# An S4D convolution with a gated feed-forward: the list scheduler replaced by one written-out order of all queues

## The chip, the cores and the metric

The kernel runs on one core of one Trainium2 chip. The metric is the device time of one execution in microseconds (us). Smaller is better. Three executions of the kernel before took 641.35, 641.83 and 646.14 us; their median is 641.83.

The core has five instruction streams that matter here: TensorE (PE, with its weight loads as PEld), VectorE (DVE), ScalarE (ACT), GpSimd (POOL) and SyncE (SP), which here mostly issues DMA transfers. Each engine runs its stream strictly in the order in which the program was built. Streams meet only at semaphores: an instruction whose input is not ready holds up everything behind it on its own engine.

## The reference

The input `x` (also `u`) has 2048 rows of 640 channels. One branch is a state-space convolution, the other a dense feed-forward of inner width 1728, and a gate per row mixes the two:

```python
dt = exp(log_dt); A = -exp(log_A_real) + 1j * A_imag
C = (C_real + 1j * C_imag) * dt[:, None]
P = exp((A * dt[:, None])[:, :, None] * pos)          # 640 x 128 x 2048
K = 2.0 * einsum("dn,dnl->dl", C, P).real             # convolution kernel
y = irfft(rfft(u_t, 2L) * rfft(K, 2L))[:, :, :L]      # causal convolution
a = y + u * D_skip
b = relu(B_x @ w1) @ w2                               # B_x: 2048 x 640
g = sigmoid((u * gate_w).sum(-1, keepdims=True))
out = g * a + (1 - g) * b
```

All inputs and the output are float32.

## The kernel before, in words

**Feed-forward.** Rows are worked on in blocks of 512 and 256. PE transposes an input block (`pk<-ident,xu`), ACT and DVE copy it out as a high part (ACT's CAST) and a low part (DVE) into the tile `xx`. Both weight matrices are split the same way, into `w1h`/`w1l` and `w2h`/`w2l`, and each product is made of three matmuls (high by high, low by high, high by low) in the accumulator `pf`, of which there are two banks. The hidden layer goes through ACT (`hh`, the ReLU) and DVE (`hl`, its low part); the second product is folded by DVE into the result tile `q`, which has two buffers. Feed-forward needs nothing of the other branch, so it is used as filler on PE from the first microsecond to the last.

**Generator.** To make the convolution kernel K, PE builds exponents in one bank (`pg<-tg,PS`, written by the visits of the queue `g`), ACT and DVE turn them into sines, cosines and magnitudes (`sc`, `mg`), DVE multiplies these into `G`, and PE contracts them into `pk` (the queue `gt`), from which DVE makes `kt`. `kt` goes through memory to `ck`. This fills the time from about 97 to 372 us.

**Convolution.** It is a Fourier transform in stages, one block of channels after another. PE's first stage is `pc<-ck,tf` for K (queue `sk`) and `pc<-xu,tf` for the input (queue `su`); the second stage is `pc<-ku,tm` and the second inverse `pc<-ku,tn` (both in the queue `s2`); the first inverse is `pc<-ku,tw` (queue `s4`). All write the accumulator `pc`, which has three banks. Between the stages DVE, ACT and POOL copy and multiply (`ku`, `kx`). After the last stage ACT empties `pc` with the gate into `yo` (two buffers), POOL adds, and transfers write the output. In the rest of this document a visit is one such task of PE.

**What sets the order.** Nothing is issued when it is written down. Every step is recorded as a task by `Plan.add` (L297), which names its engine, its queue, an estimated duration, the tasks that it depends on, the buffers that it takes (`take`) and those that it still reads (`use`). There are 2359 tasks in 57 queues. Within a queue the order is fixed. `Plan.run` (L344) then merges the queues: it keeps a model of each engine, looks at the head of every queue, and picks by rank. The rank is the one given at `add` plus a correction for each task number from the table `MOVES` (L265, made by `moves`, L135). Constants (L277 on) charge a change of kind on PE (`STICK`, and `CHANGE` in time) and the fetching of instructions (`FETCH`, `BUSY`, `STALL`). Where a task is picked its function runs and issues its instructions, so that the order of picks is the order on each engine.

All instructions are recorded by one helper (`Pinned.__getattr__`), so that the profile gives nearly all of them its line, L444; they are told apart by their tiles.

Of the kernel before, what the change touches and what calls it, by code (L numbers as in the profile page):

```python
# [25 lines left out]
S4R = 3  # L26
SKR = 2
SUR = 2
SKD = 2
SUD = 3  # L30
# [3 lines left out]
AHEAD = ()  # L34
HB = 1
XR = 2
XTR = 2
XT0 = 2
LATE_X = 1
LOGP = 0  # L40
LOGR = 3
JS2 = 0
JS1 = 0
JS4 = 0
STQ = 'SP'
STR = 4
TGR = 6
TGA = 4
TURNS = 2
G1R = 2  # L50
G4R = 3
LMR = 2
G5R = 0.5
GPR = 1
GTR = 3
S2D = 1
S2P = 2
RLR = 2
S4A = .5
PA = 3  # L60
PL = 2.5
YO = 2
YJ = 2
KRANK = 3

# [3 lines left out]

# [32 lines left out]

# [16 lines left out]
class Token:  # L119


    def __init__(self, ring):
        self.ring, self.users, self.left, self.free = ring, 0, 0, 0.0


class Ring:
    def __init__(self, n):
        self.n, self.slots = n, [0.0] * n

    def token(self):  # L130
        return Token(self)

def moves():  # L135
    r = {}
    for v, s in (
# [119 lines left out]
        for x in s.split():  # L257
            a, _, step = x.partition('/')
            a, _, b = a.partition('-')
            for i in range(int(a), int(b or a) + 1, int(step or 1)):  # L260
                r[i] = v
    return r


MOVES = moves()  # L265


# [1369 lines left out]
```

## Time and profile before

One execution was profiled. Its instructions span 642.3 us; the profile gives no other time of it. That is 0.5 above the median of the three timed runs, 641.83.

| | busy, us | share of the span | instructions |
|---|---|---|---|
| PE | 618.4 | 96% | 8676 |
| PEld | 493.1 | 77% | 8676 |
| DVE | 505.5 | 79% | 841 |
| ACT | 377.8 | 59% | 539 |
| POOL | 84.0 | 13% | 114 |

The mean clock that the throttle granted to PE is 0.992 of full. A busy PE need not be PE at its peak: matmuls are pipelined and the end of each is modelled, so rows of PE overlap, and what a matmul costs is read from the start of one row to the start of the next. In the rows a tile stands without its number, `out<-in`, with the part of the array that it uses, its shape and how many of the same kind follow each other; in brackets is the time that the engine idled just before, and what ended it. "issue" is idle time for which the profile shows no releaser.

### The profile page before, as it was taken

What the parts mean: (1) busy time and instruction counts of PE and PEld (TensorE: products, weight loads), DVE (VectorE), ACT (ScalarE), POOL (GpSimd) and SP (SyncE); (2) the same over time, 40 slices, a digit from 0 to 9 for tenths busy, and PEclk for the clock granted to TensorE, in tenths of its full rate; (3) what the DMA queues carried; (4) which work ended last, traced back from release to release, by engine and by line L of the source; (5) the groups of instructions that cost most, each with busy time, mean ns of one, the idle gap of its engine ahead of it and who ended that gap; (6) DMA issues with size and microseconds to landing.
All of it is one profiled execution on the core that took longest, in us unless ns stands there. A gap on an engine that the chain in (4) does not pass through costs nothing.

```text
span 642.3 us, 19948 instructions
## 1 busy us (share of the span) xinstructions
PE 618.4 (96%) x8676; PEld 493.1 (77%) x8676; DVE 505.5 (79%) x841; ACT 377.8 (59%) x539; POOL 84.0 (13%) x114
## 2 busy tenths in 40 slices
PE   7999999899999999999999999998999989899997
PEld 5999998888997887888898886666647645557666
DVE  4699946998999989999999957886757857858642
ACT  5455338999898987899889803131441452233541
POOL 0000000000000000000000000051340440532634
PEclk9899999999999999999999999999999999999999
DMA  9954974332346632533353269966139656454165
GB/s 241 284 221 148 277 238 139 106 110 102 109 133 210 230 128 94 199 124 108 112 187 116 79 195 261 266 144 136 32 78 271 177 155 145 174 134 135 59 187 141
DMA packets 75457, 102.56 MB, mean 160 GB/s; under 512 B 7529, under 2 KB 58601, under 8 KB 75114
## 3 DMA queue, kind: packets, MB, share of 16 engines
q1 hardware_dynamic: 74970, 100.39, 51.8%
q8 instruction: 68, 1.11, 0.7%
q10 hardware_dynamic: 400, 0.90, 0.5%
q14 instruction: 19, 0.16, 0.1%
HBM read 62.21 MB, written 39.06 MB: 158 GB/s over the span
## 4 chain that ended last, share of the span: by engine, by line
PE 60%; DVE 14%; ACT 13%; DMA 6%; issue 3%; SPq 2%; POOL 1%; DVEq 0%; ACTq 0%; POOLq 0%
PE pf L444 38%; PE pc L444 15%; ACT sc L444 5%; PE pk L444 4%; DVE sc L444 4%; DVE G L444 3%; DVE mg L444 3%; ACT L444 3%; PE pg L444 3%; SPq L444 2%; DMA out_dram<-yo 2%; ACT mg L444 2%; DMA xu<-in_A_u_dram 2%; ACT yo L444 1%; DMA part<-q 1%
## 5 line engine op out<-in xcount | busy, mean ns | idle before, releaser
L444 PE MATMUL pf<-xx,w1h 128*128 128x256 f32 (+1 forms) x760 | 190.8, 348 | 0.7 <-DVE w1h L444 0.4
L444 PEld LDWEIGHTS pf<-xx,w1h 128*128 128x128 f32 x760 | 125.5, 193 | 32.2 <-issue 16.5
L444 POOL TENSOR_TENSOR ku<-ku,kx 128x256 f32<-128x256 f32 x80 | 56.8, 735 | 488.6 <-ACT ku L444 422.4
L444 PE MATMUL pf<-xx,w1l 128*128 128x512 f32 (+1 forms) x340 | 117.1, 344 | 0.1
L444 ACT COPY ku<-pc 128x512 f32<-128x512 f32 (+1 forms) x60 | 43.9, 752 | 87.3 <-PE pc L444 87.2
L444 PE MATMUL pf<-w2h,hh 128*128 128x320 f32 x288 | 91.1, 320 | 1.2 <-issue 0.6
L444 PE MATMUL pf<-w2l,hh 128*128 128x320 f32 x288 | 87.7, 309 | 0.0
L444 DVE STREAM_TRANSPOSE ku<-pc 128x512 f32<-128x512 f32 x80 | 77.3, 1060 | 13.2 <-PE pc L444 13.0
L444 PE MATMUL pf<-w2h,hl 128*128 128x320 f32 x256 | 74.0, 315 | 0.0
L444 PEld LDWEIGHTS pf<-xx,w1l 128*128 128x128 f32 x340 | 65.7, 193 | 7.9 <-DVE w1l L444 0.3
L444 PEld LDWEIGHTS pf<-w2h,hh 128*128 128x128 f32 x288 | 54.0, 188 | 11.9 <-issue 9.2
L444 ACT ACT_TABLE_LOAD x42 | 53.9, 1283 | 4.1 <-DVE sc L444 3.3
L444 PEld LDWEIGHTS pf<-w2l,hh 128*128 128x128 f32 x288 | 54.1, 188 | 0.2
L444 DVE TENSOR_TENSOR mg<-mg,sc 128x1024 f32<-128x1024 f32 x40 | 48.9, 1223 | 2.4
L444 PEld LDWEIGHTS pf<-w2h,hl 128*128 128x128 f32 x256 | 46.3, 188 | 5.6 <-issue 5.1
L444 ACT COPY sc<-pg 128x1024 f32<-128x1024 f32 x40 | 40.4, 1010 | 16.0 <-PE pg L444 16.0
L444 DVE TENSOR_TENSOR sc<-sc,mg 128x1024 f32<-128x1024 f32 x40 | 48.8, 1219 | 0.0
L444 ACT ACTIVATE sc<-sc,half_pi 128x1024 f32<-128x1024 f32 x40 | 45.6, 1139 | 0.0
L444 ACT ACTIVATE hh<-pf 128x512 fp32r<-128x512 f32 (+1 forms) x40 | 20.3, 508 | 41.8 <-PE pf L444 41.8
L444 PE MATMUL pc<-ku,tm 64*32 64x256 f32 x1280 | 41.3, 380 | 3.4 <-issue 1.9
L444 DVE SCALAR_TENSOR_TENSOR hl<-pf,hh 128x512 fp32r<-128x512 f32 (+1 forms) x40 | 23.2, 580 | 26.6 <-ACT hh L444 15.8
L444 ACT ACTIVATE sc<-sc 128x1024 f32<-128x1024 f32 x40 | 42.2, 1055 | 0.2
(171 smaller groups left out, 1153.1 us busy)
## 6 DMA issues: line engine op xcount, KB each, us to landing
xx<-xt SPq DMA_DIRECT2D x24, 640.0 KB, 6.7
xt<-xx SPq DMA_DIRECT2D x16, 640.0 KB, 3.9
part<-q SPq DMA_DIRECT2D x16, 640.0 KB, 3.4
q<-part SPq DMA_DIRECT2D x16, 640.0 KB, 4.4
ws<-in_B_w_dram SPq DMA_DIRECT2D x20, 320.0 KB, 3.7
kd<-kt SPq DMA_DIRECT2D x80, 64.0 KB, 1.7
ck<-kd SPq DMA_DIRECT2D x40, 128.0 KB, 4.5
xu<-in_A_u_dram SPq DMA_DIRECT2D x10, 512.0 KB, 6.6
```

The source lines that it names most:

```text
L444: return lambda *a, **k: self._tc.keep_in_program_order(f(*a, **k))
```

## The change

`Plan.run` no longer decides anything. `QUEUES` gives each of the 57 queues a letter, and `ORDER` is a string that says from which queue the next task comes, with a count where several come in a row, 2359 steps in all. `run` walks through it, checks that each task's inputs are done and its buffers free in this order, and lets it issue. Durations, ranks, lags, `MOVES` and the constants are gone from the code, and `add` loses those arguments. The tasks, their dependencies, the buffers and their counts, and the order within each queue are the same, and so is the number of matmuls, vector operations and transfers. What differs is how the queues are merged.

```diff
+QUEUES = {
+    'a': 'ACT.ff', 'b': 'ACT.g', 'c': 'ACT.gw', 'd': 'ACT.mx', 'e': 'ACT.prma', 'f': 'ACT.prmc',
...
+    'B': 'DVE.z', 'C': 'PE.ff', 'D': 'PE.g', 'E': 'PE.gb', 'F': 'PE.gt', 'G': 'PE.s2', 'H': 'PE.s4',
+    'I': 'PE.sk', 'J': 'PE.su', 'K': 'POOL.mx', 'L': 'POOL.s2', 'M': 'POOL.s4', 'N': 'PY.open', 'O': 'SP.ck',
...
+ORDER = (
+    'C,N:R4,C,Ca,Cam,am,lmlAElACA3C2lCACA2amcCmC2amClmClA2CAl2CAaCamClmCAlU2CaACamCmB2CaBCB:CBCa;2C.CaQtftC2tC2tC'
...
-    def add(self, eng, q, dur, fn, deps=(), take=(), use=(), rank=5, mode=None, kb=0, port=False, n=0, late=False):
+    def add(self, eng, q, fn, deps=(), take=(), use=()):
...
     def run(self):
-        self.free = {e: 0.0 for e in self.LAG}
...
+        queues = {k: iter(self.queues.pop(tuple(x.split('.')))) for k, x in QUEUES.items()}
+        assert not self.queues, list(self.queues)
+        for n, k in re.findall(r'(\d*)(\D)', ORDER):
+            for _ in range(int(n or 1)):
+                t = next(queues[k])
+                assert all(d.done for d in t.deps), (k, n)
+                for b in t.take:
+                    b.ring.free -= 1
+                    assert b.ring.free >= 0, (k, n)
+                t.fn()
+                t.done = True
+                for b in (*t.take, *t.use):
+                    b.left -= 1
+                    b.ring.free += b.left == 0
+        assert not any(next(q, None) for q in queues.values())
```

Counted over the whole program by the queue of each task, PE's stream falls into 244 stretches of one kind before and 209 now: of feed-forward 113 and 88, of stage two and the second inverse (`s2`) 34 and 28, of `su` 16 and 14, of `sk` 14 and 11, of the first inverse (`s4`) 6 and 7; those of the generator (40 of `g`, 20 of `gt`) stay. A way from feed-forward into the convolution and back occurs 65 times before and 44 times now, one into the generator and back 46 and 42 times. The separate instructions that only wait for a semaphore are 174 and 206 on DVE, 106 and 93 on ACT, 153 and 158 on PE, 180 and 161 on SP, 87 and 90 on POOL. On SP the first weight load is now issued ahead of the first input load.

PE at the start of the program, before. `pg<-gw,ones` spreads the gate's weights over the partitions (queue `gb`), `pf<-xx,w1h` is the first hidden group of feed-forward:

```order
L444 MATMUL pg<-ident,xu 128x128 x2
L444 MATMUL pf<-xx,w1h_156 128x256 x10
L444 MATMUL pf<-xx,w1h_191 128x256 x2
L444 MATMUL pf<-xx,w1l_192 128x256
...
L444 MATMUL pk<-ident,xu 128x128 x4
L444 MATMUL pg<-gw,ones 128x512
L444 MATMUL pg<-gw,ones 128x128
L444 MATMUL pf<-xx,w1h_199 128x256 x2
```

The same place now:

```order
L186 MATMUL pg<-ident,xu 128x128 x2
L186 MATMUL pg<-gw,ones 128x512
L186 MATMUL pg<-gw,ones 128x128
L186 MATMUL pf<-xx,w1h_182 128x256 x10
L186 MATMUL pf<-xx,w1h_186 128x256 x2
L186 MATMUL pf<-xx,w1l_187 128x256
...
L186 MATMUL pk<-ident,xu 128x128 x4
```

The spreading moved from behind the next block's transposes to ahead of the first hidden group, directly behind the transposes that use the same bank `pg`.

PE in the convolution, from the second pair of first-inverse visits on (515 to 530 us of the profile), before. `tw` is the first inverse, `tn` the second, `ck,tf` and `xu,tf` the first stage of the next block of channels:

```order
L444 MATMUL pc<-ku,tw 64x512 x8
L444 MATMUL pf<-xx,w1h_5183 128x512 x2
L444 MATMUL pf<-xx,w1l_5184 128x512
L444 MATMUL pc<-ku,tn 64x128 x64
...
L444 MATMUL pc<-ck,tf 64x512 x4
L444 MATMUL pf<-xx,w1h_5210 128x512 x2
L444 MATMUL pf<-xx,w1l_5211 128x512
L444 MATMUL pc<-ck,tf 64x512 x4
L444 MATMUL pc<-xu,tf 64x512 x8
```

The same place now:

```order
L186 MATMUL pc<-ku,tm 32x256 x32
L186 MATMUL pc<-ku,tw 64x512 x4
L186 MATMUL pf<-xx,w1h_5192 128x512 x2
L186 MATMUL pf<-xx,w1l_5193 128x512
L186 MATMUL pc<-ku,tn 64x128 x64
L186 MATMUL pc<-ku,tw 64x512 x4
L186 MATMUL pc<-ck,tf 64x512 x8
...
L186 MATMUL pc<-xu,tf 64x512 x4
L186 MATMUL pc<-ck,tf 64x512 x8
```

The two first-inverse visits (`x8` is two of them) stand apart now, the second behind a feed-forward group and the second inverse, and the first-stage visits stand two and three together.

DVE in the generator, around 123 us of the profile, before. `G`, `mg` and `sc` are the generator's products, `hl` and `xx` feed-forward steps:

```order
L444 TENSOR_TENSOR kt<-kt,dsk 128x8
L444 SCALAR_TENSOR_TENSOR G<-mg,sc 128x16x32
L444 TENSOR_TENSOR G<-mg,sc 128x16x32
L444 TENSOR_TENSOR mg<-mg,sc 128x16x2x32
L444 SCALAR_TENSOR_TENSOR hl_1582<-pf,hh_1581 128x512
L444 TENSOR_TENSOR xx<-pk,xx 128x512
```

The same place now:

```order
L186 SCALAR_TENSOR_TENSOR G<-mg,sc 128x16x32
L186 TENSOR_TENSOR G<-mg,sc 128x16x32
L186 TENSOR_TENSOR kt<-kt,dsk 128x8
L186 SCALAR_TENSOR_TENSOR hl_1566<-pf,hh_1565 128x512
L186 TENSOR_TENSOR xx<-pk,xx 128x512
L186 SCALAR_TENSOR_TENSOR hl_1587<-pf,hh_1586 128x256
L186 TENSOR_TENSOR mg<-mg,sc 128x16x2x32
```

The two feed-forward steps moved ahead of the generator's product into `mg`.

At the end of the program the last two first-inverse visits of PE moved behind four more pieces of feed-forward. In the last block of channels a run of stage-two visits (`tm`) now follows a second inverse (`tn`) with nothing between.

More of the change, by code (lines that the diff above doesn't have):

```diff
@@ L1 @@
 import math
+import re
 from contextlib import ExitStack
@@ L560, in weights @@
             else:
-                a = A('SP', 'w', 1.2 if first and f else 0.62, load, after, take=[s_], kb=fn * (5 if first and f else 2.5), rank=1)
-            b = A('ACT', 'w', 0.63, high, [a], take=[w_], use=[s_], rank=1)
-            c = A('DVE', 'w', 0.75, low, [b], use=[s_, w_], rank=1, port=True)
+                a = A('SP', 'w', load, after, take=[s_])
+            b = A('ACT', 'w', high, [a], take=[w_], use=[s_])
+            c = A('DVE', 'w', low, [b], use=[s_, w_])
             wload[p, f, two] = a
@@ L870, in gates @@
             for k in range(17):
-                a = [A('DVE', 'gate', 0.16, rec.one(k, 17, go), a, rank=4)]
+                a = [A('DVE', 'gate', rec.one(k, 17, go), a)]
             self.gated = a[0]
@@ L1520, in copy @@
                         S.mul(o, st['p4', i, j][:, q, b], self.gate[:, b0 + b:b0 + b + 1])
-                c = A('ACT', 's4', 1.0, copy, [a], take=[x for x in (y_, g_ if first else None) if x],
-                      use=[b_] + ([g_] if g_ and not first else []), rank=S4A)
+                c = A('ACT', 's4', copy, [a], take=[x for x in (y_, g_ if first else None) if x],
+                      use=[b_] + ([g_] if g_ and not first else []))
                 self.need_gates.append(c)
```

409 lines of the change are left out of this document (122 added, 287 removed), and 124 rows, old and new, of tables (QUEUES, r).

## Prediction

> **What bounds the kernel now.** I read the profile in this order: the busy times and the chain of waits on the page, the busy times by stage, the table of what TensorE (PE) waited for, and then the timelines of the places that those point to. The page first: busy time and share by engine, then the chain that ended last by engine.
>
> ```profile
> PE 618.4 (96%) x8676; PEld 493.1 (77%) x8676; DVE 505.5 (79%) x841; ACT 377.8 (59%) x539; POOL 84.0 (13%) x114
> ...
> PE 60%; DVE 14%; ACT 13%; DMA 6%; issue 3%; SPq 2%; POOL 1%; DVEq 0%; ACTq 0%; POOLq 0%
> ```
>
> PE is the bound over the whole, yet 40% of the chain is something else, so one has to go by stage. The busy times in four stretches (the first loads, feed-forward alone, the stage that generates the convolution kernel, the convolution with its tail); the columns are length, then PE, weight load, DVE, ACT, POOL, clock, DMA share and GB/s:
>
> ```profile
> 0.00:23.00 23.00, 18.20 (x96) 16.07 (x97) 11.91 (x25) 10.76 (x20) 0.87 (x7) 0.85 1.01 259
> 23.00:97.00 74.00, 73.45 (x564) 72.50 (x562) 57.34 (x126) 33.96 (x71) 0.00 (x0) 1.00 0.70 225
> 97.00:372.00 275.00, 268.08 (x4255) 234.83 (x4259) 255.47 (x431) 243.81 (x273) 0.00 (x0) 1.00 0.40 134
> 372.00:640.00 268.00, 258.63 (x3784) 169.70 (x3772) 180.80 (x261) 89.28 (x176) 83.14 (x107) 0.99 0.58 161
> ```
>
> From 23 to 97 us PE is idle for 0.55 us: nothing to gain. From 97 to 372 PE (268.1 of 275), DVE (255.5) and ACT (243.8) are all nearly full, with DVE only 275 − 255.5 = 19.5 us from being the bound itself. From 372 on PE alone is full. The idle time that an order can remove is 23 − 18.2 = 4.8, 6.9 and 9.4 us in the other three. What PE waited for (total, times, longest):
>
> ```profile
> PE pc L444 <- issue: 3.6, 2, 1.9
> PE pc L444 <- ACT yo L444: 3.0, 2, 1.7
> PE pk L444 <- DVE xx L444: 3.0, 4, 1.4
> PE pk L444 <- DMA xu<-in_A_u_dram: 2.6, 2, 1.7
> PE pg L444 <- ACT mg L444: 2.4, 4, 1.2
> ```
>
> These five are 14.6 us. But a busy PE also hides what a change of kind costs, since a matmul's end is modelled and its row reads as busy. That cost shows in the starts of neighbouring rows.
>
> **Fewer changes of kind on PE.** The timeline of PE around 522 and 503 us (start, busy, instruction):
>
> ```profile
> 521.55 0.73 PE L444 MATMUL pf<-xx,w1h 128*128 128x512 f32 x2
> 522.12 0.40 PE L444 MATMUL pf<-xx,w1l 128*128 128x512 f32 x1
> 522.35 0.62 PE L444 MATMUL pf<-xx,w1h 128*128 128x512 f32 x2
> 522.81 0.40 PE L444 MATMUL pf<-xx,w1l 128*128 128x512 f32 x1
> 523.14 1.09 PE L444 MATMUL pc<-ck,tf 64*64 64x512 f32 x8
> 524.16 0.73 PE L444 MATMUL pf<-xx,w1h 128*128 128x512 f32 x2
> ...
> 502.50 1.96 PE L444 MATMUL pc<-ku,tm 64*32 64x256 f32 x64
> 504.39 0.42 PE L444 MATMUL pf<-w2l,w2h 128*128 128x320 f32 x1
> ...
> 507.67 1.09 PE L444 MATMUL pc<-ku,tm 64*32 64x256 f32 x32
> 508.69 0.74 PE L444 MATMUL pf<-xx,w1h 128*128 128x512 f32 x2
> ```
>
> Within feed-forward, two matmuls take 522.81 − 522.35 = 0.46 us from start to start; the two just after a convolution matmul take 522.12 − 521.55 = 0.57, so entering costs 0.11. A single one takes 522.35 − 522.12 = 0.23 before its like and 523.14 − 522.81 = 0.33 before a convolution visit, so leaving costs 0.10. One stage-two visit that feed-forward follows takes 508.69 − 507.67 = 1.02; two together take 504.39 − 502.50 = 1.89, so the first, with its like behind it, takes 0.87: 0.15 more. A round trip into the convolution and back is 0.11 + 0.10 + 0.15 = 0.36. By the order, the trips between feed-forward and convolution fall from 65 to 44: 21 × 0.36 = 7.6 at most. A trip whose place PE would have waited at anyway saves nothing; if that holds for two in five, 4.5 is left. Trips to the generator fall by 4 and count nothing here, with 4 × 0.36 = 1.4 as their upper bound. The waits listed above number 14 against 65 trips, so most trips don't stand at a wait: I take **−7.2**, bounds −4.5 to −9. The Trainium skill, in "TensorEngine Tiling (Array Packing)", Key Properties, says that a change of tiling mode drains TensorE; the rows agree in direction (128*128 to 64*64 and back), and the page has no price.
>
> **The start.** The timeline of PE from 11.9 to 21.6 us, with the idle time and its releaser in brackets:
>
> ```profile
> 11.91 0.28 PE L444 MATMUL pf<-xx,w1l 128*128 128x256 f32 x1
> ...
> 12.27 0.28 PE L444 MATMUL pf<-xx,w1l 128*128 128x256 f32 x1
> 14.23 0.63 PE L444 MATMUL pk<-ident,xu 128*128 128x128 f32 x4 [1.68 <-DMA xu<-in_A_u_dram]
> 14.79 1.83 PE L444 MATMUL pg<-gw,ones 1*128 1x512 f32 x4
> 16.55 0.80 PE L444 MATMUL pf<-xx,w1h 128*128 128x256 f32 x2
> ...
> 20.98 0.41 PE L444 MATMUL pf<-xx,w1l 128*128 128x256 f32 x1
> ...
> 21.62 0.41 PE L444 MATMUL pf<-xx,w1l 128*128 128x256 f32 x1
> ```
>
> The gate's broadcast takes 16.55 − 14.79 = 1.76 us and stands behind a wait of 1.68 for the next block of the input. Now it stands ahead of the first hidden group, so it fills that wait: −1.68, if its bank (written by transposes just before it, emptied by ACT and DVE) is free. On SP the first weight load is now issued ahead of the input; one issue on that queue takes about 0.6 (row below), so everything behind may come 0.6 later. After the wait a group of three matmuls takes 21.62 − 20.98 = 0.64 instead of 12.27 − 11.91 = 0.36: half the clock, for some (21.62 − 16.55)/0.64 = 8 groups, 8 × 0.28 = 2.2 us. Without the gap this should go at least in part; I take −1.9. Sum −1.68 + 0.6 − 1.9 = **−3.0**, bounds 0 to −3.9. The Trainium skill ("TensorE: Matmul & The Clock Gate", What's actually happening) lets the clock fall only after an idle window of about 3.4 us on a free-running grid. Here 1.68 us of waiting came before it, so gap and clock need not be tied as closely as I tie them; that is a rival below.
>
> **The convolution's banks.** PE at 525 us, and the two rows that bear on the tail:
>
> ```profile
> 525.05 1.09 PE L444 MATMUL pc<-ck,tf 64*64 64x512 f32 x8
> 527.83 1.95 PE L444 MATMUL pc<-xu,tf 64*64 64x512 f32 x16 [1.69 <-ACT yo L444]
> ...
> 612.57 0.62 SPq L444
> ...
> 624.57 4.59 DMA out_dram<-yo
> ```
>
> The two visits of the first inverse (pc<-ku,tw) stand together in before, take two of the three convolution banks, and ACT empties them one after the other (yo). Now a feed-forward group and two visits stand between the second and the first at this place, so ACT has the first bank empty when the second is written, and feed-forward follows before the next visit asks for a bank. Of the 3.0 us in the table I take **−2.0**, bounds −3.0 to +1. New close neighbours cost something: in the last block of channels the first stage-two visits (tm) now stand directly behind the second inverse (tn), and several stage-two visits stand in pairs where a feed-forward group lay between, so a bank or the input of a visit may come late. The trace shows no wait of such a pair; the nearest rows are the yo waits, 1.7 at the longest. One of those and half of another: **+2.5**, bounds 0 to +5.
>
> **The tail.** The last two first-inverse visits now stand behind four more pieces of feed-forward, each of three long matmuls (3 × 0.23 = 0.69): some 2.7 us later in PE's work. What hangs on them is a chain: output transfer (4.59 above), ACT, POOL, and DVE's step into q, for which PE already waits:
>
> ```profile
> PE pf L444 <- DVE q L444: 0.5, 2, 0.3
> ```
>
> So nothing covers this chain. It would end 2.7 later against PE's work, unless the visits' own transfers, which queue on SP at 0.62 an issue, find the queue emptier: **+1.3**, bounds 0 to +2.7.
>
> **The generator stage.** Around 123 us DVE does a long product of the generator ahead of the small step (xx) that PE's next transposes wait for; the first two rows are DVE's, the last is PE's:
>
> ```profile
> 122.47 1.23 DVE L444 TENSOR_TENSOR mg<-mg,sc 128x1024 f32<-128x1024 f32 x1
> ...
> 124.22 0.68 DVE L444 TENSOR_TENSOR xx<-pk,xx 128x512 fp32r<-128x512 f32 x1
> ...
> 124.95 0.44 PE L444 MATMUL pk<-ident,xu 128*128 128x128 f32 x2 [1.39 <-DVE xx L444]
> ```
>
> With the product behind xx, that wait falls by up to 1.23. xx itself needs ACT's copy, which runs beside the product:
>
> ```profile
> 122.47 0.58 ACT L444 CAST xx<-pk 128x512 fp32r<-128x512 f32 x1
> ```
>
> It ends at 123.05. DVE's hl step stays ahead of xx, and takes what lies between the two rows, 124.22 − 122.47 − 1.23 = 0.52, so that it is over before 123.05. So xx can start near 123.1 in place of 124.22: 1.0 earlier, with some room for what comes late. A second of the four waits in the table is taken to be of this kind. That is −1.9 of the 3.0. The waits for ACT's mg (2.4) fall where the generator's visits to PE, which share one bank, stand further apart; I leave the longest (1.2) as it is, since the order is the same there, and halve the rest: −0.6. Against these, DVE has 32 more waiting instructions than before (206 for 174), and behind each the generator's work queues in order: +0.5 taken. **−2.0**, bounds −4 to +2.
>
> **Instruction supply.** Two waits have no releaser but issue:
>
> ```profile
> 448.39 2.36 PE L444 MATMUL pc<-ku,tn 32*64 32x128 f32 x86 [1.75 <-issue]
> ...
> 548.56 1.75 PE L444 MATMUL pc<-ku,tm 64*32 64x256 f32 x56 [1.88 <-issue]
> ```
>
> Both break a run of small matmuls in the middle, where instructions are consumed fastest. The instruction set is the same and the small matmuls stand at nearly the same counts from the start, so I leave both: **0**, bounds −3.6 (both gone) to +3.8 (two more). The Trainium skill ("Runtime: NRT & Kernel Launch", Instruction fetch mechanics) says that fetching is hidden behind the issue of instructions; by it these waits would not be there, and denser runs would cost nothing. The rows speak against it, so longer stretches of small matmuls remain a danger.
>
> **Sum.** −7.2 − 3.0 − 2.0 + 2.5 + 1.3 − 2.0 + 0 = −10.4. The profiled execution spans 642.3 us: 642.3 − 10.4 = 631.9. The median of the runs is 641.83, 0.5 below that span, so the forecast is 631.5.
>
> **Rivals.** With this kernel about 1% (635.4 and 648.2) can be told from no change.
>
> 1. The new neighbours eat the gains of the waits. The two terms of −2.0 vanish and +2.5 and +1.3 stay: 642.3 − 7.2 − 3.0 + 3.8 = 635.9, so 635.4 as a median or a little above. For it: PE's waits move easily from one releaser to another, as five nearly equal ones show. Against: in the convolution feed-forward waits nowhere for long (of its waits only that for q, 0.3 at the longest, is shown there), so there is work to put between. Chance 0.16, within 1%.
> 2. The clock at the start stays halved, because it follows a window and not the gap. The start gives −1.1 in place of −3.0: 631.5 + 1.9 = 633.4. This is what the clock page's grid allows. Chance 0.12, faster.
> 3. Two more runs of small matmuls break for instructions: 631.5 + 2 × 1.9 = 635.3, and up to 637 with half a clock behind each. For it: longer stretches. Against: the same total in the same blocks. Chance 0.08, mostly within 1%.
> 4. Slower: DVE becomes the bound of the generator. It runs in order, and each of its 32 added waits can hold it for one ACT operation, whose mean is about 1.0 in the generator:
>
> ```profile
> L444 ACT COPY sc<-pg 128x1024 f32<-128x1024 f32 x40 | 40.4, 1010 | 16.0 <-PE pg L444 16.0
> ```
>
> 32 × 1.0 = 32 us against 19.5 us of slack: the stage grows by 12.5, its −2.0 is lost, and the gaps it opens on PE leave more feed-forward for the end. 631.5 + 12.5 + 2.0 = 646, and with the start's gain lost too 649. It decides from 0.6 us per added wait on. Against: before, 431 DVE instructions of the stage shared 19.5 us of idle time, 0.05 each, so that a wait is mostly met already. Chance 0.07, of which 0.05 slower by over 1%.
> 5. All terms near their good ends: 642.3 − 9 − 3.9 − 3 − 4 + 0 = 622.4, 624 being likelier. Chance 0.09, faster.
>
> That the change doesn't do what it says is ruled out: the order shows 209 stretches of one kind on PE where 244 were.
>
> **Numbers.** The forecast's own case has 0.48, with 628 to 635. Faster: 0.48 + 0.12 + 0.09 + a little of 1 and 3 = 0.71. Within 1%: 0.24. Slower: 0.05. The range 624 to 638.5 leaves out the slower rival, the far ends of 1, 3 and 5, and little else.
>
> **What would show it.** Right: between 10 and 20 us no wait of PE over 0.5 and the clock column at full by 20; the wait for ACT yo under 1 us in all; the wait for DVE xx near 1; the generator's end (the last pg matmul) some 5 us earlier; PE's busy time down by about 7 with the same number of matmuls. Wrong: DVE in the chain of waits well above 14%, PE waits in the generator above 7 us, a third and fourth wait for issue, or a wait of over 2 us in the last 20 us of PE.

## The result, and the profile after

The changed kernel takes 621.5 us (median of four runs, 620.6 to 622.7), the kernel before 641.7: a ratio of 0.969, 95% interval 0.965 to 0.973. It is 20.2 us faster, twice the 10.4 that were forecast, and 2.5 us below the forecast range. The profiled execution spans 619.5 us, 22.8 less than that of before. (`QUEUES` names 58 queues; the text above counts 57.) Here are the page of the kernel after (busy time by engine, then the chain that ended last), and its busy times by stage, with borders at the same places in the work as for before:

```profile
PE 605.9 (98%) x8676; PEld 492.8 (80%) x8676; DVE 505.9 (82%) x841; ACT 376.1 (61%) x539; POOL 83.9 (14%) x114
...
PE 76%; ACT 8%; DVE 7%; DMA 4%; issue 2%; SPq 1%; POOL 1%; ACTq 0%; DVEq 0%; POOLq 0%
```

```profile
0.00:23.00 23.00, 18.25 (x116) 17.02 (x117) 11.31 (x23) 12.56 (x24) 0.88 (x7) 0.93 0.95 250
23.00:94.00 71.00, 70.77 (x541) 70.15 (x540) 58.78 (x129) 31.67 (x67) 0.00 (x0) 1.00 0.60 201
94.00:362.00 268.00, 265.35 (x4242) 233.81 (x4244) 252.16 (x427) 243.26 (x273) 0.00 (x0) 1.00 0.45 144
362.00:617.00 255.00, 251.51 (x3793) 171.82 (x3785) 183.63 (x264) 88.56 (x176) 82.98 (x107) 1.00 0.61 171
```

PE's share of the chain rose from 60 to 76%: it is nearer to being the only bound. DVE does the same 506 us in a shorter time and did not become the bound of the generator. What PE waited for, after:

```profile
PE pg L186 <- DVE xx L186: 1.7, 1, 1.7
...
PE pg L186 <- ACT mg L186: 1.3, 2, 1.1
PE pk L186 <- DMA xu<-in_A_u_dram: 1.1, 1, 1.1
PE pc L186 <- issue: 1.0, 3, 0.5
PE pk L186 <- DVE xx L186: 0.9, 3, 0.5
PE pc L186 <- DVE ku L186: 0.8, 2, 0.5
PE pk L186 <- issue: 0.6, 2, 0.4
```

ACT yo is gone from the list (3.0 before), issue fell from 3.6 to 1.0 for `pc`, DVE xx for `pk` from 3.0 to 0.9.

Since both orders hold the same tasks, PE's time can be split task by task: the start of a task to the start of the next, less the shortest usual such time of tasks of the same make-up (their 5th percentile over both traces). What is left over is idle time that the trace shows, or a cost at a place where the next task is of another queue, or the rest (halved clock, and tasks that take longer than their best). In us:

| PE, us | before | after | difference |
|---|---|---|---|
| work at its usual best | 570.4 | 570.4 | 0 |
| idle: start and feed-forward alone | 3.9 | 3.5 | −0.4 |
| idle: generator | 6.9 | 2.7 | −4.3 |
| idle: convolution | 7.7 | 2.1 | −5.6 |
| changes of kind: convolution | 20.5 | 13.4 | −7.1 |
| changes of kind: elsewhere | 7.8 | 5.3 | −2.6 |
| rest | 19.2 | 16.4 | −2.8 |

The differences add up to 22.8; the 1.5 us ahead of PE's first matmul and the 4.4 from its last task on are the same in both and are left out. Some 45% of it is waits, and nearly as much is changes of kind. Of the last two rows 2.3 belong to the first 25 us, that is, to the clock (below).

### The profile page after: what moved, and what is told of

Read it like the earlier page. It is cut to its first block, busy times and chain, and to the rows that moved or that the text cites. A ratio compares the mean times of both kernels' runs of the same rounds, so it can differ in the third digit from the quotient of the medians.

```text
span 619.5 us, 19956 instructions
## 1 busy us (share of the span) xinstructions
PE 605.9 (98%) x8676; PEld 492.8 (80%) x8676; DVE 505.9 (82%) x841; ACT 376.1 (61%) x539; POOL 83.9 (14%) x114
## 3 DMA queue, kind: packets, MB, share of 16 engines
q8 instruction: 68, 1.11, 0.8%
## 4 chain that ended last, share of the span: by engine, by line
PE 76%; ACT 8%; DVE 7%; DMA 4%; issue 2%; SPq 1%; POOL 1%; ACTq 0%; DVEq 0%; POOLq 0%
PE pf L186 51%; PE pc L186 15%; PE pk L186 6%; PE pg L186 4%; ACT sc L186 4%; DVE ku L186 3%; ACT L186 2%; SPq L186 1%; ACT mg L186 1%; DMA xu<-in_A_u_dram 1%; DMA ck<-kd 1%; DVE sc L186 1%; DVE mg L186 1%; DVE G L186 1%; DMA out_dram<-yo 1%
## 5 line engine op out<-in xcount | busy, mean ns | idle before, releaser
L186 PE MATMUL pf<-xx,w1h 128*128 128x256 f32 (+1 forms) x760 | 187.0, 344 | 0.0
L186 PEld LDWEIGHTS pf<-xx,w1h 128*128 128x128 f32 x760 | 124.9, 192 | 28.0 <-issue 13.4
L186 ACT ACTIVATE mg<-pg 128x1024 f32<-128x1024 f32 x40 | 41.7, 1043 | 0.2
L186 PE MATMUL pc<-ku,tm 64*32 64x256 f32 x1280 | 39.8, 379 | 0.6 <-DVE ku L186 0.5
```

The costliest lines, as they stand in the source:

```text
L186: return lambda *a, **k: self._tc.keep_in_program_order(f(*a, **k))
```

## The experiments

All are the changed kernel's code with another `ORDER` string (the order of before can be written as such a string too), two of them with one more edit, which is shown. A ratio is to the runs of before on the same chip.

| run | what | median, us | ratio, 95% interval |
|---|---|---|---|
| e_start | changed order up to the generator only | 642.5 | 1.002 (0.998 to 1.006) |
| e_gen | changed order in the generator only | 636.1 | 0.990 (0.986 to 0.994) |
| e_conv | changed order in the convolution only | 628.5 | 0.982 (0.976 to 0.987) |
| e_loads_later | before, two loads later | 638.4 | 0.995 (0.992 to 0.998) |
| e_no_loads_before | before, four loads left out | 638.0 | 0.993 (0.990 to 0.996) |
| e_after_again | the changed kernel again | 622.5 | 0.969 (0.966 to 0.972) |
| e_no_loads_after | changed, four loads left out | 620.1 | 0.965 (0.962 to 0.968) |
| e_loads_into_runs | changed, one load behind a store | 624.6 | 0.971 (0.966 to 0.976) |
| e_load_early | changed, one load earlier | 622.8 | 0.970 (0.967 to 0.973) |
| e_resplit | changed, 21 more trips | 630.9 | 0.980 (0.976 to 0.985) |
| e_dve_back | changed, DVE's products back | 623.3 | 0.971 (0.966 to 0.976) |
| e_yo_joined | changed, one pair of visits joined | 624.8 | 0.973 (0.971 to 0.975) |
| e_tail_back | changed, the tail's visits back | 625.4 | 0.974 (0.972 to 0.977) |
| e_gate_later | changed, gate's spreading later | 621.8 | 0.968 (0.964 to 0.973) |
| e_best | changed, two places mended | 619.7 | 0.965 (0.963 to 0.967) |

### The three stages, each alone

```diff
 e_start: tasks up to the first generator visit      + changed order   then order of before
 e_gen:   from there to the first convolution visit  + changed order   order of before ahead and behind
 e_conv:  from there to the end                      + changed order   order of before ahead
```

> The order of the change up to the first generator visit (to about 94 us), the order of before from there on. Theory (the gain is a sum over places that don't depend on each other): by the two traces this part of PE's work has 3.0 us less of idle time, halved clock and changes of kind, so 641.7 - 3.0 = 638.7 us. Rival (the clock at the start follows a window of its own and not the order): the time stays within 1 us of 641.7.

Measured: 642.5, ratio 1.002. The rival holds; "The start" below shows why.

> The order of before up to the first generator visit, the order of the change through the generator (up to the first visit of the convolution), then the order of before again. Theory: the generator's part has 6.0 us less of waits and changes of kind by the two traces, 641.7 - 6.0 = 635.7 us, with the waits of PE for DVE xx and ACT mg in the generator at 2 to 3 us in place of 5. The two waits for issue of the convolution (1.75 and 1.88) are still there. Rival (DVE bounds the generator, and what PE gains there comes back as other waits): 640 to 642.

Measured: 636.1, ratio 0.990, that is 3.7 to 9 us. The theory holds: in its trace PE's idle time in the generator is 2.7 us, as after, and the three waits for issue in the convolution are there with 6.0 us in all.

> The order of before up to the first visit of the convolution, the order of the change from there on. Theory: changes of kind -7, the waits for ACT yo -3, the two long waits for issue and the halved clock behind one of them -5, 641.7 - 13.6 = 628 us with small ones. Rival (the waits for issue went only because everything stands some us earlier, so that transfers and code borders happen to miss each other): one or two waits for issue of over 1 us return, 631 to 634.

Measured: 628.5, ratio 0.982, that is 8.4 to 15 us. The theory holds. In its trace the convolution's changes of kind cost 13.7 us and its idle time is 2.6 us (20.5 and 7.7 before); no wait for ACT yo, and the longest for issue is 0.8. The two stages alone give 5.4 + 13 = 18 of the 20 us.

### The start

Five profiled executions here have the start of before, and ten that of the change. The first visit of the generator begins at 93.6, 94.0, 95.4, 96.9 and 97.4 us with the one, and between 94.1 and 96.7 with the other; both means are 95.5. The two profiles that the prediction is compared with happened to be 96.9 and 94.2, so a good part of these 2.7 us is luck. What differs is the clock. Busy times from 17 to 24 us, where the number before the last two is the granted clock: the kernel before, and then e_no_loads_before, whose order is the same there:

```profile
17.00:24.00 7.00, 7.00 (x41) 7.00 (x41) 4.18 (x8) 3.25 (x7) 0.00 (x0) 0.62 1.19 279
```

```profile
17.00:24.00 7.00, 7.00 (x59) 7.00 (x57) 7.00 (x15) 3.81 (x8) 0.00 (x0) 1.00 1.20 277
```

41 matmuls at clock 0.62, 59 at 1.00, in the same order behind nearly the same wait (1.68 and 1.54 us; e_loads_later has 1.69 and clock 1.00). The fifteen profiles sort by it. With the start of before, no stretch at half the clock after the first 9 us goes with 93.6 and 94.0, one of 3.4 us with 95.4, two with 96.9 and 97.4. With that of the change, one goes with 94.1 to 94.4 (four profiles) and two with 95.7 to 96.1 (three). In the other three PE is slow from its first matmul to 17 us, and the generator begins at 96.6 or 96.7. There the clock column reads 1.00 all the same, so the rows have to be asked. In e_start a group of three takes 16.27 − 15.63 = 0.64, as at half the clock:

```profile
15.63 0.41 PE L186 MATMUL pf<-xx,w1l 128*128 128x256 f32 x1
...
16.27 0.41 PE L186 MATMUL pf<-xx,w1l 128*128 128x256 f32 x1
```

So at the same number of slow stretches the changed start is about 1.2 us shorter. But none of its ten profiles is without one, and two of the five of before are; whether that is the order or chance, these few profiles don't settle.

And the wait that the move of the gate's spreading was to fill has moved, not gone. PE after:

```profile
9.72 1.34 PE L186 MATMUL pg<-gw,ones 1*128 1x512 f32 x4 [1.68 <-DVE xx L186]
...
13.75 0.41 PE L186 MATMUL pf<-xx,w1l 128*128 128x256 f32 x1
...
14.39 0.41 PE L186 MATMUL pf<-xx,w1l 128*128 128x256 f32 x1
```

The spreading waits 1.68 us for its own bank, which DVE empties last of three; and the groups of three behind it still take 14.39 − 13.75 = 0.64, half the clock. The next run puts it later:

```diff
 L186 MATMUL pg<-ident,xu 128x128 x2
-L186 MATMUL pg<-gw,ones 128x512
-L186 MATMUL pg<-gw,ones 128x128
 L186 MATMUL pf<-xx,w1h_182 128x256 x10
 ...
+L186 MATMUL pg<-gw,ones 128x512
+L186 MATMUL pg<-gw,ones 128x128
 L186 MATMUL pk<-ident,xu 128x128 x4
```

> The changed kernel, with the gate's spreading on PE moved behind the first hidden group, ahead of the next block's transposes, so that no matmul waits at 7.7 us for its bank. Theory (in the change the wait of 1.68 us only moved from 12.5 to 8 us): the first hidden matmuls start near 8.4 in place of 11.0, the spreading fills the wait for the input, and the transposes that start at 15.6 start near 14.4: -1.2, 620.3 us, or 619.5 if less of it runs at half the clock. Rival (the start is bound by the transfers, or the clock falls later instead): 621.5 within 0.5.

Measured: 621.8, and a wait of 1.70 us for DVE's w1h in the same place. The rival's time holds, for a reason that it didn't name: the change has also put the first weight's split behind the three xx on DVE, so the first hidden group isn't ready any sooner (11.06 us, 10.99 in the changed kernel). With both mended, and one more place:

```diff
 e_best = e_gate_later, and
+SP: first input load ahead of the first weight load (as before)
+ACT, DVE: first weight's split (w1h) ahead of the three xx (as before)
+PE: second generator visit (pg<-tg,PS) behind two more feed-forward pieces
```

> The changed kernel with two places mended. At the start the first input load and the first weight's split stand first again, as before, and the gate's spreading stands between the first hidden group and the next block's transposes; and the second generator visit stands behind two more pieces of feed-forward, so that ACT has emptied its bank. Theory: of the waits at 8 and 12 us (1.7) and at 98 us (1.1) at most 0.5 is left: 621.5 - 2.3 = 619.2 us. Rival (the clock at the start falls elsewhere in each execution and hides it): 621.5 within 1.

Measured: 619.7, five runs between 619.4 and 620.3, against 620.1 to 625.4 for the changed kernel in ten runs. PE in its start, and later in the generator:

```profile
12.31 1.34 PE L186 MATMUL pg<-gw,ones 1*128 1x512 f32 x4
14.15 0.63 PE L186 MATMUL pk<-ident,xu 128*128 128x128 f32 x4 [0.50 <-DMA xu<-in_A_u_dram]
...
99.71 0.50 PE L186 MATMUL pg<-tg,PS 32*128 32x512 f32 x4 [1.27 <-ACT mg L186]
```

The wait for the input is down to 0.5, the profile shows no stretch at half the clock behind its first 6 us, and the generator begins at 92.1 us. But the wait for mg only moved from the second visit to the third: from the first generator visit to the end of the profile it is 525.5 us, and 525.3 in the changed kernel. So what the profile gains is all in the start. The gain on the changed kernel is about 2 to 3 us by the medians; the intervals of the ratios (0.963 to 0.967, against 0.965 to 0.973 and 0.966 to 0.972) overlap a little.

### Changes of kind

```diff
-L186 MATMUL pc<-ck,tf 64x512 x8
+L186 MATMUL pc<-ck,tf 64x512 x4
 L186 MATMUL pf<-xx,w1h_5192 128x512 x2
 L186 MATMUL pf<-xx,w1l_5193 128x512
+L186 MATMUL pc<-ck,tf 64x512 x4
 (21 such places)
```

> The changed kernel, with 21 pairs of convolution visits on PE split again: where two visits and two feed-forward pieces follow each other, the second visit and the first piece change places, so that there are 65 trips between feed-forward and convolution as before. Nothing else is touched. Theory (a trip costs 0.36 us of PE, whether it stands at a wait or not): 621.5 + 21 x 0.36 = 629.1 us. Rival (a split visit gives its bank time, and most trips are free): 621.5 to 624.

Measured: 630.9, against 621.5 and 622.5 for the changed kernel: 8.4 to 9.4 more. In its trace the convolution's changes of kind cost 22.4 us in place of 13.4 and 14.0 in the two traces of the changed kernel: 8.4 to 9.0 for 21 trips, 0.40 to 0.43 each. By the ratios, each to the runs of before on its own chip, it is 7.2 us, 0.34 each. The theory holds, and its 0.36 lies between the two.

### The generator's order on DVE

```diff
 L186 TENSOR_TENSOR kt<-kt,dsk 128x8
+L186 TENSOR_TENSOR mg<-mg,sc 128x16x2x32
 L186 SCALAR_TENSOR_TENSOR hl_1566<-pf,hh_1565 128x512
 L186 TENSOR_TENSOR xx<-pk,xx 128x512
-L186 TENSOR_TENSOR mg<-mg,sc 128x16x2x32
 (and the same with two products near 147 us)
```

> The changed kernel, with DVE's long products of the generator put back ahead of the feed-forward steps hl and xx at two places (near 120 and 147 us). Theory: PE's wait for DVE xx comes back there, 1.0 us each, and nothing later gives it back, as PE is the bound: 623.5 us. Rival (the generator has slack elsewhere, DVE's own time is the bound): 621.5 within 0.7.

Measured: 623.3, 0.8 to 1.8 more than the changed kernel, in one run of four 628.2; the interval doesn't tell it from none. The trace does. PE at the two places in e_dve_back:

```profile
121.87 0.44 PE L186 MATMUL pk<-ident,xu 128*128 128x128 f32 x2 [1.49 <-DVE xx L186]
149.68 0.44 PE L186 MATMUL pk<-ident,xu 128*128 128x128 f32 x2 [2.01 <-DVE xx L186]
```

After, these waits are 0.26 and 0.07. PE's idle time in the generator is 5.0 us in place of 2.7: 2.4 more, of which 0.5 comes back in smaller costs at changes of kind. So both waits go with DVE's order, and nothing in the generator makes up for them.

### The banks and the tail

```diff
-L186 MATMUL pc<-ku,tw 64x512 x4
+L186 MATMUL pc<-ku,tw 64x512 x8
 L186 MATMUL pf<-xx,w1h_5192 128x512 x2
 L186 MATMUL pf<-xx,w1l_5193 128x512
 L186 MATMUL pc<-ku,tn 64x128 x64
-L186 MATMUL pc<-ku,tw 64x512 x4
 L186 MATMUL pc<-ck,tf 64x512 x8
```

> The changed kernel, with the second pair of first-inverse visits (the place of the prediction, 497 to 503 us in the changed kernel) put together again as before: the second visit directly behind the first, ahead of the feed-forward group and the second inverse. Theory (the pair holds two of three banks until ACT has emptied both): the wait for ACT yo is back with 1.0 to 1.7 us within the next 10 us, 623 us. Rival (the bank is free in time with the longer stretches behind it): no such wait, 621.5 within 0.5.

Measured: 624.8. A wait is back on the first stage's visit, behind the joined pair (first row) and the second inverse:

```profile
499.57 3.66 PE L186 MATMUL pc<-ku,tw 128*64 128x512 f32 x16
...
507.21 1.09 PE L186 MATMUL pc<-ck,tf 64*64 64x512 f32 x8 [1.06 <-ACT ku L186]
```

It is 1.06 us, and the profile puts it to ACT's ku, which empties a bank of the second inverse. The wait for yo of the theory is not there, and ACT isn't late. From e_yo_joined, ACT's rows at this place:

```profile
501.60 2.18 ACT L186 ACTIVATE yo<-pc,gate 128x128 f32<-128x128 f32 x8 [1.36 <-PE pc L186]
506.12 2.00 ACT L186 COPY ku<-pc 128x1024 f32<-128x1024 f32 x2 [2.34 <-PE pc L186]
```

ACT has emptied both banks of the pair at 503.78 and then waits 2.34 us for PE's second inverse. In the joined order the first stage follows that inverse directly, and its bank can be emptied only when the inverse is over; in the changed kernel a first-inverse visit stands between and covers this. So the wait is one of close neighbours, and the pair alone doesn't bring back the wait for yo. Three such pairs stand in the changed kernel too (452, 538 and 598 us), and PE doesn't wait for yo there.

Where PE did wait for yo before (510 and 526 us), ACT itself waited for the output transfers to free one of its two yo buffers. ACT in the kernel before:

```profile
509.81 1.14 ACT L444 ACTIVATE yo<-pc,gate 128x128 f32<-128x128 f32 x4 [3.28 <-DMA out_dram<-yo]
...
525.27 1.14 ACT L444 ACTIVATE yo<-pc,gate 128x128 f32<-128x128 f32 x4 [1.17 <-DMA out_dram<-yo]
526.63 1.14 ACT L444 ACTIVATE yo<-pc,gate 128x128 f32<-128x128 f32 x4 [0.22 <-DMA out_dram<-yo]
```

Such waits of ACT add up to 16.8 us before, 5.8 after and 5.1 in e_yo_joined. Which of the moves on POOL, SP or ACT lets the transfers go sooner was not tested. As to the time, 2.4 us of this profile's 3.1 above the changed kernel's lie ahead of the first generator visit (96.6 for 94.2); from there to the end it is 526.0 us, against 525.3 and 527.8 in the two profiles of the changed kernel. A cost of the joined pair beyond the one wait isn't shown.

```diff
+L186 MATMUL pc<-ku,tw 64x512 x8
 L186 MATMUL pf<-xx,w1h_5372 128x512 x2
 ... (four pieces of feed-forward)
-L186 MATMUL pc<-ku,tw 64x512 x8
```

> The changed kernel, with the last two first-inverse visits of PE moved ahead of the four feed-forward pieces that they stand behind in the change. Theory of the prediction (the chain behind them has no cover at the end): the end comes up to 2.7 us sooner, 620.2 us. Theory after the result (the chain is over before the last feed-forward pieces, and the end is set by PE alone): 621.5 within 0.5, with the same 3.9 us from the last matmul to the end of the span.

Measured: 625.4, slower by 2.9 to 3.9, so neither theory holds. The last matmul ends 3.9 us ahead of the end in both, but PE waits on the way; 1.9 of the 3.9 between the two profiles lie ahead of the first generator visit (96.1 for 94.2), and 2.0 behind it. From e_tail_back, rows of PE, of DVE, and of ACT:

```profile
608.46 0.42 PE L186 MATMUL pf<-w2h,hh 128*128 128x320 f32 x1 [2.09 <-DVE q L186]
```

```profile
607.85 1.01 DVE L186 SCALAR_TENSOR_TENSOR q<-pf,omg,q 128x320 f32<-128x320 f32 x2 [3.70 <-POOL q L186]
```

```profile
602.83 0.60 ACT L186 ACTIVATE w2h<-pf 128x512 fp32r<-128x512 f32 x1 [3.19 <-PE pf L186]
603.32 0.83 ACT L186 ACTIVATE q<-q,omg 128x640 f32<-128x640 f32 x1
604.04 2.17 ACT L186 ACTIVATE yo<-pc,gate 128x128 f32<-128x128 f32 x8
```

PE did the visits early, but the changed order on ACT has the last hidden block's ReLU ahead of yo (its result is kept in the tile w2h, which is free by then). That ReLU needs the four feed-forward pieces, which now come later. So yo starts at 604.04 where it started at 599.73 after, POOL and DVE follow, and PE waits 2.09 us. Before, ACT had the two the other way round:

```profile
621.33 2.17 ACT L444 ACTIVATE yo<-pc,gate 128x128 f32<-128x128 f32 x8 [3.85 <-DMA out_dram<-yo]
623.46 0.60 ACT L444 ACTIVATE w2h<-pf 128x512 fp32r<-128x512 f32 x1
```

The moves on PE and on ACT belong together. What the pair of moves is worth against the order of before was not tested.

### Instructions

The page has 68 packets of 1.11 MB on the instruction queue, 16 KB each, and 8676 matmuls with as many weight loads: about 128 of each to a packet. So the place where PE enters a new block can be counted off, to some ten instructions, and the trace has the start of the packet that is fetched when it does. (The scheduler of the kernel before already reckons with fetches that transfers delay: `block` in `run` takes `FETCH`, 3.55 us, plus `BUSY`, 0.5 us for each us that transfers are still under way.) The kernel before enters one at 441.5 us. DMA traffic from 441.6 to 446.0, and from 446.0 to 447.5:

```profile
q1 hardware_dynamic: 1345, 0.92, 115.5%
```

```profile
q8 instruction: 1, 0.02, 4.4%
q1 hardware_dynamic: 16, 0.02, 3.3%
```

No instruction packet moves until the two-part load of xu (512 KB a part by the page; the expectations below have it too small), issued at 437.9, is over at 446.1. The fetch is 4.5 us late, and PE waits 1.75.

```diff
 SP, order of before:
-DMA xu<-in_A_u_dram (at 437.9 and at 538.9 us)
+DMA xu<-in_A_u_dram (behind what SP issues near 462 and 556 us)
```

> The order of before, with two loads of the convolution's input (the two-part loads of xu, 640 KB, that SP issues at 437.9 and 538.9 us) issued later, near 462 and 556 us; PE's order is untouched. Theory (the next block of PE's instructions isn't fetched until such a load is nearly over): the waits for issue of 1.75 and 1.88 us go, and with the first the halved clock at 449 to 452: -5.2, 636.5 us. Rival (the small matmuls of these runs use up instructions faster than they can ever be fetched): both waits stay, 641.7 within 1.

Measured: 638.4, ratio 0.995, 1.2 to 5 us. The loads were issued at 441.6 and 545.0, less late than meant. The two long waits are gone, and so is the halved clock; the fetches at these two borders begin 1.4 and 0.9 us after the border where it was 4.5 and 4.6. One wait of 1.1 us stands near 559, after the second load has ended; what it comes from isn't shown. So the theory holds as to the two waits, with a smaller gain.

```diff
 SP, changed order; the second load keeps its place in SP's queue:
-DMA xu<-in_A_u_dram (434.7 us)
 DMA part<-q
+DMA xu<-in_A_u_dram
```

> The changed kernel, with the same two loads of xu issued some 5 to 7 us later (near 440 and 540 us in place of 434.7 and 532.8), so that each is under way when PE enters its next block of instructions, at 442.1 and 541.6, in a run of small matmuls. PE's order is untouched. Theory (a load delays the fetch): a wait for issue of about 2 us near 447 and one of 3 to 4 near 545, perhaps with a halved clock behind: 621.5 + 5 = 626.5 us, between 624 and 630. Rival (the changed order's runs are short enough for any fetch): 621.5 within 1.

Measured: 624.6. It tells nothing. On SP only the first load moved, behind one store. The loads were issued at 437.1 and 535.7 with everything else some 2.5 us later too, so that they stood where they had stood. The wait of 1.8 us that it shows near 547 the unchanged order can show as well:

```profile
547.50 0.45 PE L186 MATMUL pc<-ku,tn 32*64 32x128 f32 x8 [1.84 <-issue]
```

This is e_after_again; in the first profile of the same order the wait here is 0.25.

```diff
+L186 DMA xu<-in_A_u_dram 64x16x128 x2
 L186 DMA xx<-xt_66 128x1280 x2
-L186 DMA xu<-in_A_u_dram 64x16x128 x2
```

> The changed kernel, with the last two-part load of xu (640 KB, issued at 532.8 us) issued as soon as its buffer is free, ahead of another load that SP waits for: near 520.5 us. PE enters its next blocks of instructions at 521.8 and 526.6, in a run of small matmuls. Nothing on PE or elsewhere is moved. Theory (while such a load is under way the fetch of the next block isn't begun): a wait for issue of 2 to 3.7 us near 526, perhaps with half the clock behind it, and less than before at 541: 624 us, between 623 and 627. Rival (fetches are late at random, or for the density of the matmuls alone): no wait there, 621.5 within 1.

Measured: 622.8, no more than the changed kernel. The load is issued at 519.6, the border comes at 520.9, and a wait for issue of 0.74 appears at the end of the block that PE has then, near 526. The fetch begins 3.0 us after the border where it was 0.6; but that is 4 us before the load is over. So the theory is right in kind and too strong in size: a fetch doesn't always wait for the end of a load.

```diff
-                for h in range(2):
+                for h in range(0 if i else 2):
                     D_.dma_start(t[64 * h:64 * h + 64], ud[:, 16 * h:16 * h + 16, i * C:i * C + C])
```

> The order of before, without the two-part loads of xu for the second to the fifth block of channels (four of five loads, 640 KB each): their first stage reads the first block's input again. All other instructions are there, in the order of before. Theory (these loads hold the fetch of PE's next block of instructions): the waits for issue in the convolution, 4.2 us in all in the profiled execution of before, fall under 1, and the halved clock behind one of them goes: 642 - 3.5 to 5 = 637 to 638.5 us. Rival (runs of small matmuls outrun any fetch): two waits of 1.7 to 1.9 us stay, 642 within 1.5.

> The order of the change, without the same four loads of xu. Theory: little is left to gain, as the waits for issue are 1.0 to 1.6 us in all: 620.5 to 621.5 us, with the wait near 544 (0.25 us, and 0.5 to 2.3 in other executions of this order) gone. Rival (the changed order gains elsewhere and still pays for the loads): 618 or less.

> The order of the change, unchanged, as a second execution with its own profile beside the two above. If the start gains nothing but by the clock's window, the first generator visit begins anywhere between 94 and 97.5 us, and the median is 621.5 to 623.5; if the order sets the clock at the start, it begins at 94.2 again.

Measured: 638.0, 620.1 and 622.5. The theories hold in time; of the waits one of 1.4 is left where all were to fall under 1. PE's waits for issue without the loads, in the order of before, and then in that of the change:

```profile
PE pc L444 <- issue: 3.6, 2, 1.9
```

```profile
PE pc L186 <- issue: 1.4, 1, 1.4
PE pk L186 <- issue: 0.8, 1, 0.8
```

```profile
PE pc L186 <- issue: 0.3, 2, 0.2
```

The first of these three is the kernel before with its loads, for comparison. The same borders, in the same order, with the load under way and without it, as delay of the fetch behind the border:

| border | with the load, us | without, us |
|---|---|---|
| order of before, the border at 441.5 | 4.6, 4.4, 4.4 | 1.4 (moved), 1.2 (left out) |
| order of before, at 541.2 | 4.6, 3.9, 4.9 | 0.9 (moved), 1.2 (left out) |
| changed order, at 411.0 | 4.5, 4.7, 4.8 | 1.1 (left out) |

In the last row the border lies among long matmuls, so that the count can be off by a us or two, equally in both columns. The loads delay the fetches: that is settled by this table. How much of a delay becomes a wait depends on the work that PE has left in its block. In the changed order the latest fetch is at 411 us, where PE has some 7 us of work in its block, and nothing waits. In that order four loads cost about 2 us, which the intervals don't tell from none, in that of before 4 to 5. One wait of 1.4 us near 579 in the order of before stands with no such load beside it; what it is stays open.

The fall in these waits is not a matter of one pair of profiles: PE's waits for issue are 4.5, 4.8 and 6.7 us in all in the three profiles with the convolution of before, and 0.4 to 2.5 in the eleven with that of the change (or a variant) and its loads. The halved clock is such a matter: behind such a wait it stands in one of the three (before, 0.50 from 449.0 to 452.4 us, behind 1.75) and in three of the eleven (e_after_again, 0.51 from 548.6 to 552.0, behind 1.84).

e_after_again begins the generator at 95.7 us, in between: the order alone doesn't set the clock at the start.

## Why the prediction was wrong

The sign was right, and so were the mechanisms of the changes of kind and of DVE's order in the generator; the start, the banks, the tail and the instructions were not. Each was looked at, and the sum was half of what came.

- **Fewer changes of kind, −7.2.** Measured −7.1 in the convolution, and −1.4 in the generator, where nothing was counted and 1.4 was the bound. Right; the price of a trip is 0.34 to 0.43 by the experiment, 0.36 was taken.
- **The start, −3.0.** Wrong: 0 in the mean, about −1.2 at the same clock. The step that failed is "Without the gap this should go at least in part". The clock halves or doesn't, in the same order behind nearly the same gap, and the wait had only changed its releaser. The condition that the prediction set, the bank being free, isn't met: PE waits 1.68 for it. And the broadcast takes 10.99 − 9.72 = 1.27, so it couldn't fill 1.68; the 1.76 read off the trace held some of the halved clock, which is counted again in the −1.9. Rival 2 had it. The Trainium skill ("TensorE: Matmul & The Clock Gate", What's actually happening) has the activity window free-running. The trace agrees in this, with 0.62 and 1.00 in one order; its idle window of about 3.4 us isn't borne out, as the waits ahead of the half clock last 1.7 to 1.8 us.
- **The banks, −2.0 and +2.5.** The waits for yo are gone: 3.0 here, 1.7 to 3.0 in the five profiles with the convolution of before. The mechanism behind the −2.0 failed: "The two visits of the first inverse (pc<-ku,tw) stand together in before, take two of the three convolution banks". A joined pair brings no wait for yo back, and ACT had been waiting for output transfers. The cost of new neighbours is 0.8 (DVE ku), not 2.5: that step charged them with waits of the old kind's length.
- **The tail, +1.3.** Wrong: 0; from PE's last matmul to the end it is 4.0 before and 3.9 after. The step that failed is "So nothing covers this chain". It followed PE's order only. ACT's order at this place had changed with it, and the visits moved behind pieces that ACT's order wants first anyway; undone on PE alone, PE waits 2.1.
- **The generator, −2.0.** Mis-sized: −4.3 of idle time. The two places on DVE are worth 1.2 and 1.9 of waits by the experiment (1.49 − 0.26 and 2.01 − 0.07), where 1.9 was counted for both, and the many waits under 0.5, which weren't counted, went too. The 32 added waits on DVE (+0.5) cost nothing to be seen, and the slower rival built on them is refuted: DVE has 7% of the chain, not more than 14.
- **Instruction supply, 0.** The largest miss: 4.4 us of waits for issue before (all rows), 1.6 after, and the halved clock behind the first, some 1.7, which is luck. The step that failed is "the small matmuls stand at nearly the same counts from the start, so I leave both". It looked at PE alone. Most of the waits came from loads on another queue, and the change moved them against the blocks' borders. The Trainium skill's rule ("Runtime: NRT & Kernel Launch", Instruction fetch mechanics) that fetching is hidden is not borne out here: 4.6 us of delay, 1.88 of wait.

Against the forecast, in this pair of profiles, the instructions gave 4.5 more (2.8 and 1.7), the banks 2.7 (−2.2 for +0.5), the generator 2.3, the changes of kind and the tail 1.3 each. With the start at 0 (3.0 less) that is 9.1 of the 10.0 that lie between 631.5 and 621.5. The two profiles differ by 22.8, which is 12.4 more than forecast, since the second one also began its generator 2.7 earlier. Of the signs that were named, the wait for yo is gone, that for DVE xx is 0.9, and of those named for a wrong forecast only further waits for issue appeared, five in all, of 0.54 at most. But the generator's last visit comes 9.0 us earlier, not 5, and PE's busy time is down by 12.5, not 7.

## What to carry to other kernels

An order is worth what it is on all engines together: a move on one engine has to be read beside the same place on those that feed it and empty its banks, and undoing it on one alone misleads. Where the start depends on the clock, compare profiles from a place behind it. A wait put down to an engine has to be followed to what that engine waited for. Price a change of kind by start-to-start differences; that held within a fifth. Before a wait is called the same because the engine's own stream is, look for what arrives late from elsewhere, instructions too: place long loads where the engine's block of instructions holds long work.

## What the runs showed of the hardware that was not expected

- A load in two parts of 512 KB, 8.2 us long, held up the fetch of PE's next 16 KB of instructions. Where a border came 1.3 to 5.4 us after the load's issue, the fetch began 3.0 to 4.9 us after the border, against 0.6 to 1.4 at the same borders without it. Where the border came within some half microsecond of the issue, the fetch got ahead (0.6 at 435.2 us after, with the load issued at 434.7).
- The same instructions behind a wait of 1.5 to 1.8 us ran at half the clock in some executions and not in others: 93.6 to 97.4 us to the same place, with 0 to 2 slow stretches of 3.4 us. In the middle of the kernel waits of 1.75 and 1.84 us were followed by one such stretch, and one of 1.88 was not. e_best (0.9 us of waits for issue, no slow stretch after the first 6 us of its profile) spread by 1.0 us over its runs, the changed kernel by 5; but e_dve_back, also with 0.9 us, spread by 5.8, so what makes the spread isn't shown.
